# Last stage of a decode forward-and-backward kernel: last dq's products and output 1 ahead of the remaining dW units, dW spread evenly, K tiles reloaded first, later first wq load, padded rows

## The chip, the cores and the metric

One Trainium2 chip, one of its cores. The metric is the time of one execution on the device, in microseconds; a kernel's figure is the median of its runs. A small difference is read from a 95% interval; a kernel and the kernel before ran in the same rounds on the same chip. Each profile is of one run; its span is about 2 us shorter than that run's time.

## The reference, cut to what matters

```python
# two layers of attention with the same weights and caches, two MLPs between and after; one token, batch 2
x = x + attn(layernorm(x), k_cache, v_cache, wq, wo)      # caches [2, 4, 16384, 128], 32 query heads
x = x + mlp(layernorm(x), w1, b1, w2, b2)                 # 1024 -> 3584 -> 1024
x = x + attn(layernorm(x), k_cache, v_cache, wq, wo)
x = x + mlp(layernorm(x), w1, b1, w2, b2)
# outputs: x, and the gradients (vjp with grad_out) of x, k_cache, v_cache, wq, wo, w1, b1, w2, b2; all bf16
```

The big outputs are the gradients of both caches and of four weights. With one token, a weight gradient is an outer product of short rows: "dW" below. Output 1 is the gradient of x: two rows of 1024.

## The kernel before: the parts the change and the argument touch

The change is in the last stage, which begins at about 735 us: the backward pass of the first attention layer. It loads the caches again, computes ds and dq from them, and writes dK, dV and all dW. Its work is cut into steps `m`, two half-chunks of scores each. A step also takes some dW units from two queues, `fill` (MLP weights and wo) and `late` (wq). A unit is one matmul of 4 x 128 by 4 x 512, and one copy of its 128 x 512 result from PSUM into a tile ("home"); the last unit of a tile stores it.

```python
def load_tile():
    return (by_store or by_read).popleft()      # a tile whose store must land first, or one that was only read

def store(out_ap, view, tile_):
    nc.gpsimd.dma_start(out_ap, view)
    by_store.append(tile_)
# ... cut ...
fill.extend(dw_units(rowsA, rowsB, 2, list(w_chunks(HD, D)), 0, D, rows_of(out_5)))   # row group 2 of PE, last in fill
# ... cut ...
def step_fill(n):
    for k in range(n):
        for q in ((late, fill) if k % 2 == 0 else (fill, late)):
            if q and q[0].ready():
                q.popleft()()
                break

def fixed_tp(i):                                # a PSUM bank, zeroed by ACT
    t = pt([128, 8, 128], BF16, "tpm%d" % i)
    S.copy(out=t[:].bitcast(F32), in_=zero1[:].to_broadcast([128, 512]))
    return t
# ... cut: opening of the stage ...
TP.extend(fixed_tp(i) for i in range(2))
pump(NLD + 3, 4)
while 2 * m < NS + 12 or late or fill or late_pe or m <= max(v_at) + 2:
    # ... cut: transposes, scores, dK and dV pairs of the step ...
    step_fill(1 if m < NCH else 5)
    pump(NLD + 3 if m < NCH else NLD, 3)        # the next loads
    m += 1
g0 = attn_in_bwd(0, g1, dn0)                    # layer-norm backward, then output 1
col_to_row_f32(g0, DJ, out_1.rearrange("b s d -> (b s) d"), "o1")
```

## Time and profile before

| | before |
|---|---|
| median (lowest to highest) | 1144.22 us (1143.81 to 1147.24) |
| span of the profiled run | 1140.8 us |
| PE busy | 84% |
| bytes moved, mean rate | 449.3 MB, 394 GB/s |
| mean granted PE clock | 0.847 |

The page of the kernel before: busy tenths of PE's clock and of the DMA engines in 40 slices of 28.5 us, and the sum of the transfers.

```profile
PEclk9989785597999876999998899989779868896785
DMA  9999999998999989999999999887999999999996
DMA packets 89130, 449.30 MB, mean 394 GB/s; under 512 B 7026, under 2 KB 7026, under 8 KB 49788
```

The DMA engines are the limit nearly everywhere. The slices of lower share in the last stage are its opening (slices 26 to 28) and its end (the last). The same kernel, the busy time of each engine in stretches of the last stage; the last three columns are granted PE clock, DMA share and GB/s.

```profile
core 0: us, PE busy (x) PEld busy (x) DVE busy (x) ACT busy (x) POOL busy (x), PEclk, DMA share, GB/s
735.00:790.00 55.00, 45.87 (x777) 32.57 (x777) 41.15 (x77) 38.96 (x76) 5.92 (x11) 0.94 0.75 287
790.00:1110.00 320.00, 287.82 (x3682) 175.32 (x3680) 245.86 (x429) 228.93 (x440) 47.78 (x81) 0.80 1.02 420
1110.00:1120.00 10.00, 7.42 (x53) 3.79 (x52) 5.80 (x12) 4.89 (x9) 1.04 (x2) 0.50 0.83 348
1120.00:1130.00 10.00, 8.85 (x92) 3.96 (x92) 5.94 (x11) 6.06 (x11) 1.83 (x3) 0.50 0.50 206
1130.00:1140.00 10.00, 2.85 (x11) 1.19 (x10) 3.24 (x12) 0.68 (x2) 1.31 (x2) 0.50 0.59 237
```

There are three parts: an opening with holes, a full stretch at 420 GB/s, and a tail with holes, through which PE has half its clock. The holes of the tail do not mean that DMA had stopped being the limit. Each transfer adds 16 to a semaphore, one for each DMA engine (Trainium skill, "DMA: Bandwidth & Descriptors", Why a DMA increments its semaphore by 16 and not by 1: the engines finish independently, and only the full 16 means that all landed). Counting these increments in the trace, the store that was issued at 1111.86 us has its fifteenth at 1120.78 and its sixteenth at 1128.12; and stores land (sixteenth) at 1128.12, 1130.64, 1133.14, 1135.65 and 1138.13, every 2.5 us. I read this as one engine that is behind all others, works without a gap and ends the kernel; I call it the straggler. The 2.5 us agree with an engine at the common rate: a store is 1024 KB, so 64 KB for each of 16 engines, and at 420 / 16 GB/s that takes 2.5 us (an estimate).

The timeline of PE in the tail of the kernel before: start, length, group, and in brackets the idle time before it with what ended it.

```profile
1116.45 1.01 PE L1097 MATMUL tpm<-ident,dq_all 128*4 128x128 bf16 x8 [0.61 <-DVE dq_all L900]
...
1124.98 5.27 PE L1162 MATMUL xm<-rowsA,rowsB 4*128 4x512 bf16 x12 [0.49 <-ACT keepK L163]
...
1132.85 1.01 PE L200 MATMUL o<-identf,gA 128*2 128x128 f32 x4 [1.30 <-DVE gA L908]
1134.63 1.01 PE L200 MATMUL o<-identf,gA 128*2 128x128 f32 x4 [0.77 <-DVE o_row L201]
```

The last dq becomes rows at 1116.45, the last 12 dW units run at 0.44 us each, and output 1 comes after them, while the last stores still drain. And in the opening, PE waits for ACT's zeroing copy:

```profile
741.98 0.61 PE L1414 MATMUL tpm<-ident,keepxV 128*128 128x128 bf16 x8 [1.65 <-ACT tpm L1342]
```

### The profile page before, as it was taken

The numbers are of one execution on the slowest core, as the hardware profiler recorded it, in microseconds if no ns is written. First come the engines' busy times: TensorE is split into PE (matmuls) and PEld (weight loads), VectorE is DVE, ScalarE is ACT, GpSimd is POOL, SyncE is SP. The second block draws the span as 40 slices with busy tenths as digits, with TensorE's granted clock in tenths as the row PEclk, the third lists the DMA queues.
The fourth block names the chain that finished last, engine by engine and source line by source line (L and its number), as shares of the span: only waits on it lengthen the run. The fifth ranks groups of instructions, "written<-read, shape, count | busy, mean of one in ns | idle before, by whom it ended". The sixth has DMA issues, their size and how long they took to land. (4 is left out here: it accounts for less than half of the span.)

```text
span 1140.8 us, 39972 instructions
## 1 busy us (share of the span) xinstructions
PE 954.6 (84%) x17567; PEld 736.6 (65%) x17567; DVE 633.4 (56%) x1347; ACT 566.2 (50%) x1418; POOL 64.7 (6%) x117
## 2 busy tenths in 40 slices
PE   4988896487879885899987789988898989999885
PEld 3867674387767765888776688765555555555552
DVE  1535442133545433544845355768678868786784
ACT  0534351022535330344554444668677767776673
POOL 0000000000000000000000000001111112111111
PEclk9989785597999876999998899989779868896785
DMA  9999999998999989999999999887999999999996
GB/s 371 424 424 424 425 423 413 408 379 354 423 424 424 425 302 424 410 377 407 373 423 419 349 354 355 314 331 309 400 423 422 421 420 422 423 422 421 424 419 247
DMA packets 89130, 449.30 MB, mean 394 GB/s; under 512 B 7026, under 2 KB 7026, under 8 KB 49788
## 3 DMA queue, kind: packets, MB, share of 16 engines
q1 hardware_dynamic: 72204, 348.17, 75.4%
q0 software_dynamic: 16752, 98.59, 20.8%
q8 instruction: 137, 2.24, 0.7%
q14 instruction: 37, 0.30, 0.1%
HBM read 348.14 MB, written 98.58 MB: 392 GB/s over the span
## 5 line engine op out<-in xcount | busy, mean ns | idle before, releaser
L155 ACT COPY kT<-tp 128x512 int32<-128x512 int32 x209 | 122.8, 587 | 252.0 <-PE tp L421 243.3
L158 DVE COPY kT<-tp 128x1024 bf16<-128x1024 bf16 x159 | 108.6, 691 | 109.2 <-PE tp L421 97.3
L421 PE MATMUL tp<-ident,kv_K 128*128 128x128 bf16 x1728 | 144.5, 233 | 4.5 <-DMA kv_K<-in_A_k_cache_dram 4.4
L421 PEld LDWEIGHTS <-kv_K 128*128 128x128 bf16 x1728 | 109.6, 104 | 5.3 <-DMA kv_K<-in_A_k_cache_dram 5.2
L166 DVE CAST big<-xm 128x512 bf16<-128x512 f32 x135 | 88.1, 686 | 25.3 <-PE xm L1162 11.7
L163 ACT CAST big<-xm 128x512 bf16<-128x512 f32 x162 | 88.3, 594 | 24.6 <-PE xm L1162 12.7
L574 PEld LDWEIGHTS <-kT 128*128 128x128 bf16 x2048 | 76.6, 98 | 27.8 <-issue 21.4
L574 PE MATMUL sc<-qT_bf,kT 128*128 128x8 bf16 x2048 | 92.0, 171 | 0.3 <-issue 0.3
L538 ACT ACTIVATE e_all<-sc,negm 128x64 bf16<-128x64 f32 x256 | 77.1, 345 | 1.1 <-DVE negm L533 1.0
L307 PEld LDWEIGHTS <-wt 128*128 128x128 bf16 x1696 | 49.2, 104 | 43.7 <-issue 14.8
L421 PE MATMUL tp<-ident,kv_V 128*128 128x128 bf16 x864 | 70.1, 227 | 8.5 <-DMA kv_V<-in_A_v_cache_dram 7.6
L271 PE MATMUL wtp<-ident,wt 128*128 128x128 bf16 x928 | 73.9, 225 | 3.7 <-issue 2.5
L166 DVE CAST keepK<-xm 128x512 bf16<-128x512 f32 x91 | 59.1, 686 | 21.7 <-PE xm L1244 17.7
L453 PE MATMUL acc_all<-kv_V,e_all 128*16 128x256 bf16 x864 | 46.5, 296 | 26.4 <-DMA kv_V<-in_A_v_cache_dram 13.7
L163 ACT CAST keepK<-xm 128x512 bf16<-128x512 f32 x105 | 56.8, 594 | 23.8 <-PE xm L1244 23.1
L158 DVE COPY wT<-wtp 128x1024 bf16<-128x1024 bf16 (+1 forms) x64 | 40.7, 641 | 46.6 <-PE wtp L271 43.5
L155 ACT COPY wT<-wtp 128x512 int32<-128x512 int32 (+1 forms) x60 | 34.3, 572 | 61.7 <-PE wtp L271 47.5
L421 PEld LDWEIGHTS <-kv_V 128*128 128x128 bf16 x864 | 55.4, 102 | 10.7 <-DMA kv_V<-in_A_v_cache_dram 8.3
L166 DVE CAST keepV<-xm 128x512 bf16<-128x512 f32 (+1 forms) x80 | 52.5, 686 | 16.3 <-PE xm L1244 12.8
L163 ACT CAST keepV<-xm 128x512 bf16<-128x512 f32 (+1 forms) x93 | 50.3, 593 | 20.1 <-PE xm L1244 18.2
L538 ACT ACTIVATION_READ_ACCUMULATOR e_all<-sc,negm 128x1 f32 x256 | 60.1, 235 | 0.0
L271 PEld LDWEIGHTS <-wt 128*128 128x128 bf16 x928 | 56.3, 100 | 4.4 <-issue 3.0
(350 smaller groups left out, 1786.9 us busy)
## 6 DMA issues: line engine op xcount, KB each, us to landing
kv_K<-in_A_k_cache_dram SPq DMA_DIRECT2D x81, 1024.0 KB, 12.3
kv_V<-in_A_v_cache_dram SPq DMA_DIRECT2D x81, 1024.0 KB, 12.1
out_dram<-big POOLq DMA_DIRECT2D x36, 1024.0 KB, 18.5
wt<-in_A_wo_dram SPq DMA_DIRECT2D x32, 1024.0 KB, 10.2
wt<-in_B_w_dram SPq DMA_DIRECT2D x32, 896.0 KB, 14.2
out_dram<-keepK POOLq DMA_DIRECT2D x21, 1024.0 KB, 18.3
out_dram<-keepV POOLq DMA_DIRECT2D x19, 1024.0 KB, 15.0
wt<-in_A_wq_dram SPq DMA_DIRECT2D x16, 1024.0 KB, 9.0
```

What stands on the lines that cost most here:

```text
L155: S.copy(out=dst.bitcast(I32), in_=src.bitcast(I32))
L158: V.tensor_copy(out=dst, in_=src)
L163: S.copy(out=dst, in_=src)
L166: V.tensor_copy(out=dst, in_=src)
L271: PE.transpose(tp[:, o, :], wv[:, j, (o0 + o) * 128:(o0 + o + 1) * 128], ident[:])
L307: PE.matmul(fps[:, jo, :].rearrange("p (a b) -> p a b", b=2), lhsT=wv[:, j, jo * 128:(jo + 1) * 128], rhs=xT_bf[:, j0 + j, :].unsqueeze(1) ...
L421: PE.transpose(tp[:, j, :], cv[:, b * 8 + j, :], ident[:])
L453: PE.matmul(self.acc[cg:cg + 16, :], lhsT=coef(u), rhs=self.cv[:, t:t + 2, :].rearrange("p t d -> p (t d)"), start=False, stop=True, tile_ ...
L538: S.activation(out=e_all[:, g, f * half:(f + 1) * half, l, h, :], in_=sc[g][f][:, h, :].rearrange("p (a b) -> p a b", b=2), func=ACT.Exp, ...
L574: PE.matmul(sc[g][f][:, :, t % TH], lhsT=kT[:, j, :], rhs=q_bf[:, g, :], start=True, stop=True)
```

## The change: intent and diff

The intent: give the loads an earlier start in the opening (reload into K tiles, which no store holds; load wq later; drop two copies that PE waits for), and have dW units left to fill the tail's holes while the last quarter of dq goes to its products with wq and to output 1 first. The diff is cut to its core; instruction counts on PE are equal (17567 both).

```diff
+    opening = {"on": True}
     def load_tile():
-        return (by_store or by_read).popleft()
+        return (by_read or by_store if opening["on"] else by_store or by_read).popleft()
@@ loads of wq @@
-            if i % (2 * NCH) == NCH:
+            if i % (2 * NCH) == NCH + (2 if i < 2 * NCH else 0):
@@ last quarter: products with wq and output 1 at once, between the steps @@
+    def in_rows(q, kv):
+        # cut: two parts of 32 matmuls each, then layer-norm backward and output 1, one a half-step
     def quarter(kv):
         quarters[kv][1]()
-        late_pe.append(quarters[kv][3])
-        late.append(rows_unit({3: (dq_all, kv * 8)}, rowsA, kv * 8))
-        late.extend(dw_units(rowsB, rowsA, 3, [(0, 4), (4, 4)], kv * D, D,
+        if kv == order[-1] % HKV:
+            while late_pe:
+                late_pe.popleft()()
+            tail.extend(in_rows(quarters[kv], kv))
+        else:
+            late_pe.append(quarters[kv][3])
+        late.append(rows_unit({3: (dq_all, kv * 8, HQ)}, rowsA, kv * 8))
+        late.extend(dw_units(rowsB, rowsA, 3, [(0, 4), (4, 2), (6, 2)], kv * D, D,
@@ dW spread @@
-    def step_fill(n):
+    def step_fill(n, keep):
-                if q and q[0].ready():
+                if q and (q is late or len(q) > keep) and q[0].ready():
-        step_fill(1 if m < NCH else 5)
+        step_fill(1 if m < NCH else 3 if not late and 2 * m < NS else 5, 24 if 2 * m < NS else 0)
@@ opening @@
-    TP.extend(fixed_tp(i) for i in range(2))
+    TP.extend(pt([128, 8, 128], BF16, "tpm%d" % i) for i in range(2))
-    pump(NLD + 3, 4)
+    pump(NLD + 3, 3)
+    opening["on"] = False
@@ end @@
-    g0 = attn_in_bwd(0, g1, dn0)
-    col_to_row_f32(g0, DJ, out_1.rearrange("b s d -> (b s) d"), "o1")
# cut: tiles of columns padded by 7, so that 32 columns are transposed instead of 4;
# the last chunk's dq one slot earlier; late_pe popped sooner when over 6
```

## The prediction

> **What bounds the kernel now.** The page: DMA engines 90% busy or more in nearly every slice, 449.3 MB at a mean of 394 GB/s against about 424 when full; PE 84%. The change touches the last stage, from about 735 us. The windows view shows three parts there: 735 to 790, an opening with DMA share mostly 0.6 to 0.9 (229 to 367 GB/s); 790 to 1116, full (420 GB/s); and 1116 to 1138, a tail whose share falls to 0.06 from 1120 to 1125.
>
> 0.06 is one engine of 16. The trace's semaphore updates agree: from 1060 us on each store's last increment comes 6 to 13 us after its fifteenth. The last stores land at an even 2.5 us spacing up to 1138.1 us, straight through the stretch where the other engines are idle. So one straggling DMA engine has no gap from about 784 us to the end, and it ends the kernel. The Trainium skill ("DMA: Bandwidth & Descriptors", Latency and other measured facts) says that engines 7 and 15 are usually slower; the trace does not number engines, but one slow engine agrees.
>
> **What the change does.**
> - Tail: the last 24 dW units (3 MB) are held back until scores end; the last quarter's wq products and output 1 go ahead. In the before, PE and the copies stand in a chain of waits from 1104 to 1125, and 15 DMA engines idle about 6.5 us (from the GB/s of those slices). The change fills that. But the straggler is not idle there, and its bytes are unchanged. I expect the hole to vanish and little from it in the end time: 0 to 1 us, plus 0.2 us for the output-1 transfer, which now lands 0.2 us after the last big store.
> - Opening: four K/V reloads now go into K tiles, free after the dq products (736 to 740 us); before they queued behind stores (issued 740.7, 748.1, 748.6, 749.0). No DMA engine was busy for 5.1 us between 730 and 790, 2.3 of them before 750. The two bank-zeroing ACT copies go, worth the 1.65 us that PE waited at 742. Later loads still wait for stores, and compute limits the opening, so: 2 to 4 us.
> - Even spreading (3 units a step instead of 5): bytes unchanged; steps already DMA-bound (6.4 us each, against 5.5 when DMA was idle at 780). About 0.
> - Padding, memsets: 32 weight columns instead of 4, same matmul; eight small memsets under loads already queued. 0.
>
> **Prediction.** 1144.2 - 3 (opening) - 1 (tail) - 1 (fewer stalls) = 1139 us; 8 in 10 between 1130 and 1145. Faster by over 2%: 0.04; within 2%: 0.95; slower: 0.01. If the straggler did not count, the average engine's work would end the kernel near 1126 (an estimate), so 2% is nearly out of reach.
>
> **What would show it.** Right: DMA share near 1 until 2 to 3 us before the last landing; no 0.06 stretch; no PE wait on the zeroing copies; four loads issued before 742; the last stores again spaced 2.5 us, last increment several us after the fifteenth; output 1 stored before the last dW. Wrong: last stores landing within 1 us on all engines (straggler not the limit, gain 10 us or more); or compute issuing the last store only as its predecessors land (32 units in a row at 0.43 us each, PE at half clock), which ends later than the straggler.
>
> **What would make it wrong.** The straggler's extra work depending on how loads and stores overlap; the opening losing bytes with three units a step; PE throttled harder in the denser tail.

## The result, and the profile after

The changed kernel took 1147.25 us in the median (1145.53 to 1148.24, 4 runs); the kernel before, beside it, 1144.01 (1143.66 to 1147.24, 4 runs). The ratio is 1.002, with an interval of 0.9999 to 1.0042. A ratio is the mean time of one kernel's runs over that of the other's of the same rounds, so it is not quite the ratio of the two medians. The prediction was 1139, with 8 in 10 between 1130 and 1145: the measured time lies above that.

The page of the changed kernel, the same rows:

```profile
PEclk9988895597989975899998899998799688867965
DMA  8999999998999989999999999988999999999977
DMA packets 89194, 449.30 MB, mean 392 GB/s; under 512 B 7090, under 2 KB 7090, under 8 KB 49852
```

The bytes are the same; the two last slices have a lower share. The same stretches of the last stage, in the changed kernel:

```profile
735.00:790.00 55.00, 47.24 (x729) 32.20 (x726) 39.68 (x74) 36.79 (x71) 4.78 (x9) 0.88 0.84 321
790.00:1110.00 320.00, 276.89 (x3696) 168.75 (x3693) 239.62 (x427) 225.96 (x431) 48.24 (x82) 0.82 1.00 411
1110.00:1120.00 10.00, 7.89 (x99) 3.74 (x99) 6.28 (x13) 5.37 (x10) 1.30 (x2) 0.50 0.34 137
1120.00:1130.00 10.00, 7.70 (x31) 2.07 (x29) 7.95 (x17) 5.49 (x11) 2.56 (x4) 0.50 0.73 306
1130.00:1140.00 10.00, 7.42 (x18) 2.23 (x16) 6.23 (x10) 5.63 (x10) 3.00 (x4) 0.50 0.80 324
1140.00:1146.00 6.00, 0.00 (x0) 0.00 (x0) 0.00 (x0) 0.00 (x0) 0.00 (x0) 0.50 0.43 175
```

The opening moves more (321 GB/s for 287), as meant. The hole of the tail has not gone: it has moved ahead to 1110 to 1120 (137 GB/s), and after it DMA runs at 306 and 324 GB/s, below its 420, up to the end. PE in the tail of the changed kernel:

```profile
1106.83 1.03 PE L1101 MATMUL tpm<-ident,dq_all 128*32 128x128 bf16 x8 [0.62 <-DVE dq_all L904]
...
1123.84 1.01 PE L199 MATMUL o<-identf,gA 128*2 128x128 f32 x4 [0.77 <-DVE o L200]
1124.79 0.60 PE L1174 MATMUL xm<-rowsA,rowsB 4*128 4x512 bf16 x1
1124.79 0.60 PE L1174 MATMUL xm<-rowsB,rowsA 4*128 4x512 bf16 x1
...
1130.02 7.41 PE L1174 MATMUL xm<-rowsB,rowsA 4*128 4x512 bf16 x17
```

The dq rows come 9.6 us sooner than before and output 1 about 11 us sooner (1123.84 for 1134.63), but then 32 dW units are still to be done, from 1124.79 to 1137.43, the last 17 of them one after the other at 7.41 / 17 = 0.436 us. The chain that ended last says the same in one line:

```profile
1126.06 9.62 PE xm L1174 x24
```

The store counts show that the straggler is no longer the limit: it has caught up at 1116.76, and from there the sixteenth increment of every store follows the fifteenth within 0.12 us. No store was issued between 1106.25 and 1115.99; the last was issued at 1138.70 and landed at 1143.25. In the kernel before the last dW store was issued at 1131.17.

In the opening four loads are issued at 734.16 to 737.80, where before they were at 740.65 to 749.04 (about 1.5 us of this is that the stage begins sooner in this run). So the loss does not seem to be there; the traces put it at the end, and the experiments test that.

### The profile page after: what moved, and what is told of

Same layout as the page of the kernel before. It is cut to its first block, busy times and chain, and to the rows that moved or that the text cites. A ratio compares the mean times of both kernels' runs of the same rounds, so it can differ in the third digit from the quotient of the medians. Undisturbed runs are those within 1.5% of the kernel's fastest.

```text
span 1145.3 us, 40004 instructions
## 1 busy us (share of the span) xinstructions
PE 948.4 (83%) x17567; PEld 729.7 (64%) x17567; DVE 631.5 (55%) x1356; ACT 565.8 (49%) x1415; POOL 67.3 (6%) x121
## 4 chain that ended last, share of the span: by engine, by line
PE 49%; DMA 32%; DVE 9%; ACT 4%; issue 4%; POOL 0%; SPq 0%; POOLq 0%; DVEq 0%; ACTq 0%
DMA kv_V<-in_A_v_cache_dram 13%; PE tp L420 9%; PE wtp L270 5%; PE acc_all L452 4%; PE tpm L1445 4%; PE xm L1174 3%; PE xm L1256 3%; DMA wt<-in_A_wo_dram 3%; DMA kv_K<-in_A_k_cache_dram 3%; DMA wqt<-in_A_wq_dram 3%; PE turn L322 2%; PE sc L573 2%; DMA out_dram<-big 2%; DMA keepxV<-in_A_v_cache_dram 2%; PE dp L1311 2%
## 5 line engine op out<-in xcount | busy, mean ns | idle before, releaser
L161 ACT CAST big<-xm 128x512 bf16<-128x512 f32 x150 | 82.5, 593 | 33.6 <-PE xm L1256 16.5
L164 DVE CAST big<-xm 128x512 bf16<-128x512 f32 x124 | 80.6, 684 | 29.5 <-PE xm L1256 12.4
L164 DVE CAST keepV<-xm 128x512 bf16<-128x512 f32 (+1 forms) x106 | 68.9, 684 | 21.5 <-PE xm L1256 14.4
L270 PE MATMUL wtp<-ident,wt 128*128 128x128 bf16 x928 | 77.3, 232 | 3.7 <-issue 2.3
L161 ACT CAST keepV<-xm 128x512 bf16<-128x512 f32 (+1 forms) x115 | 62.3, 593 | 31.7 <-PE xm L1256 25.5
L306 PEld LDWEIGHTS <-wt 128*128 128x128 bf16 x1696 | 48.8, 103 | 43.8 <-issue 14.8
L452 PE MATMUL acc_all<-kv_V,e_all 128*16 128x256 bf16 x864 | 46.5, 295 | 26.5 <-DMA kv_V<-in_A_v_cache_dram 13.2
L270 PEld LDWEIGHTS <-wt 128*128 128x128 bf16 x928 | 59.1, 104 | 4.4 <-issue 3.1
L164 DVE CAST keepK<-xm 128x512 bf16<-128x512 f32 x77 | 49.8, 683 | 14.7 <-PE xm L1256 8.8
L1256 PEld LDWEIGHTS <-blk 32*128 32x128 bf16 x992 | 24.8, 95 | 47.6 <-issue 36.9
```

Of the source, the lines that this page charges most:

```text
L161: S.copy(out=dst, in_=src)
L164: V.tensor_copy(out=dst, in_=src)
L270: PE.transpose(tp[:, o, :], wv[:, j, (o0 + o) * 128:(o0 + o + 1) * 128], ident[:])
L306: PE.matmul(fps[:, jo, :].rearrange("p (a b) -> p a b", b=2), lhsT=wv[:, j, jo * 128:(jo + 1) * 128], rhs=xT_bf[:, j0 + j, :].unsqueeze(1) ...
L452: PE.matmul(self.acc[cg:cg + 16, :], lhsT=coef(u), rhs=self.cv[:, t:t + 2, :].rearrange("p t d -> p (t d)"), start=False, stop=True, tile_ ...
L1256: PE.matmul(pss[r][:, b * 256:(b + 1) * 256], lhsT=blk[32 * r:32 * r + 32, o + 2 * h + b, :], rhs=Qm[32 * r:32 * r + 32, :, :].rearrange(" ...
```

## The experiments

All are of five rounds; the change itself has four runs on each side. At a threshold of 2%, before_act is slower, opening_act is unclear, and all others count as the same as the kernel before; smaller differences are read from the intervals. The five rounds' kernel before took 1146.06, 1145.62, 1143.18 and 1142.41 us in the four batches, so only ratios are compared across batches; 0.001 is 1.1 us.

| run | what it is | median, us | ratio to before (95%) |
|---|---|---|---|
| the change | | 1147.25 | 1.0020 (0.9999 to 1.0042) |
| opening_only | opening and padding alone | 1141.48 | 0.9963 (0.9944 to 0.9982) |
| tail_only | the change without its earlier loads (zeroing copies still gone) | 1149.01 | 1.0026 (1.0010 to 1.0041) |
| pace5_keep0 | the change at 5 units a step | 1144.63 | 0.9997 (0.9975 to 1.0018) |
| pace5_keep24 | 5 a step, 24 held back | 1153.45 | 1.0066 (1.0040 to 1.0092) |
| pace_only | before at 3 units a step | 1146.56 | 1.0016 (0.9991 to 1.0041) |
| opening_pace | opening and 3 units a step | 1145.28 | 1.0022 (0.9997 to 1.0048) |
| pace2 | the change at 2 units a step | 1153.29 | 1.0097 (1.0064 to 1.0130) |
| keep0_chain_last | pace5_keep0, output 1 last again | 1143.54 | 0.9997 (0.9975 to 1.0019) |
| opening_zero | opening_only with the zeroing copies | 1146.94 | 1.0024 (1.0002 to 1.0046) |
| nozero_only | before without the zeroing copies | 1142.12 | 0.9990 (0.9972 to 1.0008) |
| after_mix | the change, three row groups dealt in turn | 1154.47 | 1.0076 (1.0050 to 1.0102) |
| after_mix2 | the same, bias units kept early | 1158.19 | 1.0130 (1.0107 to 1.0152) |
| before_act | before, stores on ACT's queue | 1176.54 | 1.0257 (1.0226 to 1.0287) |
| opening_act | opening_only, stores on ACT's queue | 1171.20 | 1.0227 (1.0199 to 1.0256) |
| opening_sp_tail | opening_only, last stores on SP's queue | 1141.27 | 0.9973 (0.9947 to 0.9999) |

### Which half loses: opening or tail

Theory A: the dW units left over make the tail longer than the straggler. Theory B: the loss is in the opening or the full stretch.

opening_only puts the old tail and pace behind the new opening:

```diff
-        step_fill(1 if m < NCH else 3 if not late and 2 * m < NS else 5, 24 if 2 * m < NS else 0)
+        step_fill(1 if m < NCH else 5, 0)
# and the last quarter, the wq stores of (0, 4), (4, 4), and output 1 as before
```

> The changed kernel's opening and padding alone: K tiles reloaded first, first wq load later, no zeroing copies, padded rows; tail and pacing as before. Theory A: a little faster than before, 1142 to 1143 us (from the straggler's backlog, which stands about 1.3 us earlier in the changed kernel), against the 3 us predicted. Theory B: as slow as the changed kernel, about 1147.

It has the lowest ratio: 1141.48 us, 0.9963, below both the kernel before and the change. Its last stores land at 2.5 us spacing again (1129.60, 1132.10, 1134.63, 1137.10), the last with 1.7 us between fifteenth and sixteenth: the straggler is the limit there.

tail_only is nearly its complement (the zeroing copies stay out in both):

```diff
-    opening = {"on": True}
+    opening = {"on": False}
# and the first wq load and pump as before
```

> The changed kernel with the opening of before (store tiles reloaded first, wq load at its old place; zeroing copies still gone). Theory A: loses the opening's gain and keeps the tail's loss: 1148 to 1149 us. Theory B (opening to blame): about 1144.

1149.01, ratio 1.0026, with the straggler caught up at 1118.2 and the last store issued at 1141.26. Theory A was close in both: 1141.48 for 1142 to 1143, 1149.01 for 1148 to 1149. Theory B falls: the half that it blames is the half that gains.

### How many units are left over

```diff
# pace5_keep0
-        step_fill(1 if m < NCH else 3 if not late and 2 * m < NS else 5, 24 if 2 * m < NS else 0)
+        step_fill(1 if m < NCH else 5, 0)
# pace5_keep24
+        step_fill(1 if m < NCH else 5, 24 if 2 * m < NS else 0)
```

> The changed kernel with the dW pacing of before (5 units a step, none held back); everything else of the change stays. Theory A (the tail is on PE: with 3 units a step 38 dW units are left when the scores end, 55 with the last quarter's, at 0.43 us each at half clock): only 17 units are left, the end goes back to the straggling DMA engine, about 1142.5 us, 4 to 5 below the changed kernel, and the last store's 16th increment again comes over 1 us after its 15th. Theory B (the loss lies in the opening or in the saturated stretch, the tail is innocent): stays at about 1147.

1144.63: no unit is left when the scores end, and the last store's sixteenth increment comes 1.12 us after its fifteenth, as theory A said. The gain is smaller than it said: the ratio, 0.9997, is 0.0023 below the change's (about 2.6 us for 4 to 5), with intervals that overlap, and it is not that of the opening alone. So this run by itself does not settle the matter.

> The changed kernel with 5 units a step, but 24 held back until scores end. Theory A: 41 units in the tail instead of 55, 14 x 0.43 = 6 us less PE there, so about 1141 to 1142 us (not below the straggler's end). Theory B: stays at about 1147. If holding back in itself costs, this one is slower than the run without it by 24 x 0.43 less what idle time it fills.

1153.45: theory A as I had put it missed this by over 11 us. The last case of the expectation is nearer: against pace5_keep0 it is slower by 0.0069, 7.9 us, of 24 x 0.43 = 10.3. Theory A had expected that 24 units would be a good filling for the hole. In the trace the hole stays (44 GB/s from 1120 to 1130), for two reasons. Ten of the units held back run before the dq rows, and the rows come late, at 1116.92 where pace5_keep0 has them at 1111.84 (part of these 5 us is older: its loads were 2 us later already at 730). PE in pace5_keep24:

```profile
1103.67 1.61 PE L1174 MATMUL xm<-rowsB,rowsA 4*128 4x512 bf16 x5
...
1109.22 2.31 PE L1174 MATMUL xm<-rowsB,rowsA 4*128 4x512 bf16 x5
...
1116.92 1.03 PE L1101 MATMUL tpm<-ident,dq_all 128*32 128x128 bf16 x8 [0.54 <-DVE dq_all L904]
```

And from the rows to the last landing of a dW store it takes 32.0 us (1116.92 to 1148.90), in pace5_keep0 26.4 (1111.84 to 1138.20). In the changed kernel, with 38 left, it is 36.4 (1106.83 to 1143.25).

```profile
1111.84 1.03 PE L1101 MATMUL tpm<-ident,dq_all 128*32 128x128 bf16 x8 [0.54 <-DVE dq_all L904]
```

Not all of these units run after the rows: in each of the two kernels ten of those left over run before. Counted in the traces, 16 units follow the rows in pace5_keep0, 30 in pace5_keep24 and 44 in the changed kernel. So 14 more cost 5.6 us and 28 more cost 10.1 us: 0.40 and 0.36 us for each. Units do not fill the hole for nothing, each is paid for.

The number left is not the whole of it: pace5_keep24 leaves fewer units over than the change and is slower (1.0066 for 1.0020). Its rows come at 1116.92, those of the change at 1106.83: the slower pace also makes the rows come sooner, and gives back part of what the tail costs.

A doubling should then show it far outside the spread:

```diff
# pace2
-        step_fill(1 if m < NCH else 3 if not late and 2 * m < NS else 5, 24 if 2 * m < NS else 0)
+        step_fill(1 if m < NCH else 2 if not late and 2 * m < NS else 5, 24 if 2 * m < NS else 0)
```

> The changed kernel with 2 dW units a step instead of 3. Counted while the program is built: 72 units are left when the scores end, instead of 38. Theory A (each unit left costs 0.3 to 0.44 us of copies and PE in the tail, less what the chain gains by starting earlier): 6 to 12 us slower than the changed kernel, about 1153 to 1159, with the last store issued 6 us or more later than the 1138.7 us there. If the tail is filled anyway (the units left cost nothing): within 2 us of the changed kernel.

Ratio 1.0097, 0.0077 above the change: about 8.8 us for 34 more units left, 0.26 us each (0.13 to 0.39, from the two intervals). The time fell in the range expected. Its last store was issued at 1141.29, only 2.6 us later than in the changed kernel, so that part missed; the profiled run was one of its fastest (span 1147.8; its runs lie between 1146.94 and 1160.48), so the 8.8 us do not show in this one trace. In it the rows come at 1096.23, 10.6 us sooner than in the changed kernel, and 78 units follow them; from the rows to the last landing it takes 49.6 us, 23.3 more than in pace5_keep0 for 62 more units, 0.38 us each. PE and DMA in the tail of pace2:

```profile
1110.00:1120.00 10.00, 8.59 (x32) 0.50 0.74 300
1120.00:1130.00 10.00, 10.00 (x25) 0.50 1.00 403
1130.00:1140.00 10.00, 10.00 (x25) 0.50 0.81 331
```

The same stretch in the timeline:

```profile
1118.44 21.93 PE L1174 MATMUL xm<-rowsB,rowsA 4*128 4x512 bf16 x51
```

For 22 us PE does nothing but 51 units of one row group, 21.93 / 51 = 0.43 us each, at half clock, and never idles.

### The pace or the reordering

pace_only has the change's `step_fill` and nothing else of it; opening_pace has the opening too.

```diff
# pace_only: on the kernel before
-        step_fill(1 if m < NCH else 5)
+        step_fill(1 if m < NCH else 3 if not late and 2 * m < NS else 5, 24 if 2 * m < NS else 0)
# opening_pace: the same edit on opening_only
```

> The kernel before with one thing of the change: 3 dW units a step instead of 5 while no late ones wait, and the keep of 24 (which never binds at that pace: 38 units are left when the scores end). Theory A (the change loses by the dW units that the slower pace leaves for the end, one after the other on PE at half clock): slower than the kernel before by 3 to 7 us, last stores landing on all engines within 1 us of one another, the last store issued after 1136 us. Rival B (the loss comes from the reordered last quarter and output 1, not from the pace): within 2 us of the kernel before, and the straggling engine still ends it, with lags of several us.

1.0016, between what the two theories had asked for; the time alone does not decide. The trace does: the stores issued from 1121.13 on land on all engines within 0.06 us of one another, the last dW store issued at 1135.78, so in this run the tail had turned from the straggler's to compute's, as A says.

> The opening and padding, and the pace of 3 a step (38 units left), but the last quarter, its stores and output 1 as in the kernel before. If the pace alone turns the opening's gain (ratio 0.9963) into the change's loss (1.002): 1.000 to 1.003. If the reordering does it: 0.996 to 0.998, like the opening alone. Output 1 comes last here, after all dW units.

1.0022, against 0.9963 for the opening alone and 1.0020 for the whole change. opening_pace differs from opening_only in the pace alone, by 0.0059 (0.0027 to 0.0091, about 6.7 us), and their intervals do not meet. In its trace the straggler has caught up at 1117.43, and the stores issued from 1118.55 on land on all engines within 0.09 us. So the pace by itself turns the opening's gain into the change's loss.

On the kernel before, the same pace cost only 0.0016. That fits an end that is the later of two, the straggler's and compute's: the opening moves the straggler's end, and once compute's is the later one, that gain no longer counts (with the pace, opening_pace is at 1.0022 beside pace_only's 1.0016, and tail_only, without the earlier loads, at 1.0026 beside the change's 1.0020). These differences lie inside the intervals, so this is argued and not shown.

Is the reordering free? keep0_chain_last has the products early but output 1 at the end, at 5 a step:

```diff
-            tail.append(lambda: col_to_row_f32(g0, DJ, out_1..., "o1", ...))
-        return [lambda: part(0), lambda: part(4), last]
+        ending.append(last)             # run after the loop; last() stores output 1 itself
+        return [lambda: part(0), lambda: part(4)]
```

> pace5_keep0 (1144.63) with the layer-norm backward and output 1 moved back behind all dW units; the last quarter's wq products still go at once. Theory C (output 1 first puts a chain of dependent waits ahead of the last dW units, where before it ran for free while the last stores drained): back to the opening alone, 1141 to 1142.5, last big store issued 3 to 4 us sooner than in pace5_keep0 (1134.0). Rival (the cost is in the early products and the smaller dWq stores): 1144 to 1145.

The last big store was issued at 1130.21, 3.8 us sooner than in pace5_keep0, as theory C said; but the time did not follow, 0.9997 both times. With the store sooner the straggler was the limit again (2.7 us between fifteenth and sixteenth at the end). So theory C is not borne out as a cause of time. Whether the reordering costs anything stays open: with the opening and 5 a step it measured +0.0034 (0.9963 to 0.9997, intervals that overlap), with 3 a step -0.0002.

### What the opening's gain is made of

```diff
# opening_zero: on opening_only
+        S.copy(out=t[:].bitcast(F32), in_=zero1[:].to_broadcast([128, 512]))      # for both banks
# nozero_only: on the kernel before
-    TP.extend(fixed_tp(i) for i in range(2))
+    TP.extend(pt([128, 8, 128], BF16, "tpm%d" % i) for i in range(2))
```

> The opening and padding alone (1141.5), with the two bank-zeroing ACT copies put back. Their share of the opening's gain of about 4 us: the prediction put 1.65 us of PE waiting on them. If they count fully: 1143. If the reloads into K tiles are all of it (DMA busy sooner, the copies hidden under them): 1141.5.

1.0024: the two copies, 0.6 us each on ACT, cost the opening its whole gain, and by the means more (0.0061, about 7 us, with intervals of 2 us on either side of each). The trace shows how a small delay grows. PE in opening_zero, the group that waits, and PE's busy time, clock, DMA share and GB/s after it:

```profile
743.94 0.61 PE L1452 MATMUL tpm<-ident,keepxV 128*128 128x128 bf16 x8 [1.65 <-ACT tpm L1379]
```

```profile
735.00:790.00 55.00, 47.34 (x703) 0.81 0.72 281
744.00:752.00 8.00, 7.68 (x90) 0.57 1.01 424
```

The same stretches of opening_only:

```profile
735.00:790.00 55.00, 47.63 (x771) 0.91 0.83 317
744.00:752.00 8.00, 7.39 (x144) 1.00 1.01 423
```

In these 8 us PE did 90 matmuls in the one and 144 in the other. In opening_only the first of these transposes stands at 742.33, 1.6 us sooner; by a later group of transposes (749.87 and 753.25) it is 3.4 us. The net loss of the wait is smaller than its 1.65 us, which I had overlooked: in opening_only PE waits 1.35 us for DVE right after its first group, so that the second group stands at 744.30 in the one and at 744.87 in the other, 0.6 us apart. The rest of the 3.4 us comes while the clock is at half.

```profile
744.30 0.62 PE L1445 MATMUL tpm<-ident,keepxV 128*128 128x128 bf16 x8 [1.35 <-DVE dl_rest L871]
744.87 0.84 PE L1452 MATMUL tpm<-ident,keepxV 128*128 128x128 bf16 x8 [0.32 <-ACT tpm L1379]
```
Both have the same loads in flight (issued 737 to 741 us), but the next store goes out at 756.13 in the one and at 759.51 in the other, and the DMA engines find less to do: no engine was busy for 2.9 us of 735 to 790 in opening_only, for 8.5 us in opening_zero. That the clock falls after idle time agrees with the Trainium skill ("TensorE: Matmul & The Clock Gate", What's actually happening), which says that the clock is either half or full and is set by how busy PE was over windows of about 3.4 us; here it fell to half for about 7 us, though the wait is shorter than such a window. The page calls the windows free-running, so that a wait of 1.65 us tips it may be a matter of phase. Over all 17 profiled kernels, the clock fell between 740 and 752 us in all four that have the copies (the kernel before, pace_only, opening_zero, before_act), and in two of the 13 that do not (the changed kernel, 0.72 from 740 to 744, and after_mix2, 0.57 from 744 to 748). So the copies go with the fall, but are not its only way. Nor does the clock tell the two kernels of this document apart: over 735 to 790 it is 0.94 in the kernel before and 0.91 in opening_only, whose clock falls later, from 772 to 788.

> The kernel before without its two bank-zeroing ACT copies; nothing else. In the trace of opening_zero the copies delayed the first transposes by 1.6 us, the PE clock then fell to half from about 744 to 752 us, and the steps were 3.4 us late by 753. If the copies are all of the opening's gain: ratio 0.995 to 0.998, and PE at full clock from 744 to 752. If the reloads into K tiles are needed as well: 0.999 to 1.001.

0.9990 (0.9972 to 1.0008), as expected if the reloads are needed as well. PE kept its full clock from 744 to 752 (the windows below), but the loads went out late as before, and DMA stood at 275 GB/s there. That the reloads make no gain while the copies stay is shown by opening_zero. That dropping the copies makes none without the reloads is less sure: the interval reaches to 0.9972 and meets that of opening_only (0.9944 to 0.9982), and over 735 to 790 DMA moved about as much as there (315 GB/s for 317). I think that the early reloads keep DMA fed only if compute is there to issue the stores that follow; this is argued and not shown.

```profile
735.00:790.00 55.00, 46.71 (x799) 0.91 0.80 315
744.00:752.00 8.00, 7.67 (x152) 1.00 0.75 275
```

### Does one row group limit the units

In the trace of the changed kernel units of different row groups start together (1124.79 twice), units of the same one do not. That agrees with the Trainium skill ("TensorE: Matmul & The Clock Gate", Why this matters for your kernels), which says that small-K matmuls in distinct row groups run concurrently. The copies of a unit, in the changed kernel from 1124 to 1139:

```profile
L161 ACT CAST big<-xm 128x512 bf16<-128x512 f32 x10 | 5.8, 586 | 2.0 <-PE xm L1174 2.0
L164 DVE CAST big<-xm 128x512 bf16<-128x512 f32 x10 | 6.8, 690 | 2.1 <-PE xm L1174 2.1
```

ACT and DVE together can take a unit every 1 / (1/0.586 + 1/0.690) = 0.317 us. So dealing the units among row groups should take the last stretch from 0.436 to 0.317 at best.

```diff
# after_mix: on the change
     units = [dw_units(rowsA, rowsB, 0, ...),
-            dw_units(rowsB, rowsA, 1, ...)]
+            dw_units(rowsB, rowsA, 1, ...),
+            dw_units(rowsA, rowsB, 2, list(w_chunks(HD, D)), 0, D, rows_of(out_5))]
# after_mix2: also the two bias units ahead of all dW units
```

> The changed kernel, but the dW units of the output projection are dealt among those of the two MLP weights, so that the 38 units left at the end come from three different row groups of PE in turn and no longer from one. Same number of units left, same bytes. If those units are limited by PE taking one row group at a time (17 of one group took 7.41 us, 0.44 us each, where two of different groups started together): 3 to 6 us faster than the changed kernel (1147.25), about 1142 to 1144, and the tail's DMA rate rises above 306 GB/s. If the tail is limited by the copies out of PSUM or by the homes coming free: within 1.5 us of the changed kernel.

> after_mix again without its confounder (there the two bias units, nine one-row matmuls, had slid to the very end and cost 4.4 us): here they come before all dW units. The dW units of three weights are dealt in turn, so of the 38 left when the scores end, 30 change row groups. In the changed kernel 17 units of one row group ran at 0.436 us each; ACT and DVE copies of 0.586 and 0.69 us allow 0.317 us a unit (worked out from those two). If PE's one-row-group runs limit the last stretch: 2 to 4 us faster than the changed kernel, 1143.5 to 1145.5, and the last store issued 2 to 3 us sooner after output 1 than the 12.8 us there. If not: 1147, same distance.

Both missed: 1.0076 and 1.0130, slower. In after_mix the nine bias matmuls had slid to the very end, at 4.4 us. after_mix2 mends that, and after output 1 it does 33 units in 12.1 us, 0.37 each, where the changed kernel did 32 in 12.6, 0.40 each; so the stretch itself ran a little faster, but by 1 us and not by the 2 to 4 expected. The changed kernel had already alternated in the first 15 of its 32 units, and after_mix2 still ends on nine of one group. But its dq rows come at 1116.68, 9.9 us later than in the changed kernel:

```profile
1116.68 1.04 PE L1101 MATMUL tpm<-ident,dq_all 128*32 128x128 bf16 x8 [0.54 <-DVE dq_all L904]
...
1142.57 3.99 PE L1174 MATMUL xm<-rowsB,rowsA 4*128 4x512 bf16 x9
```

Its transfers are slower in the opening (291 GB/s for 321) and the loads later from there. Three weights in turn keep three half-filled tiles instead of two, which could starve the loads of tiles; that is argued and not shown.

### The straggler and the store queue

```diff
 def store(out_ap, view, tile_):
-        nc.gpsimd.dma_start(out_ap, view)
+        nc.scalar.dma_start(out_ap, view)                          # before_act, opening_act
+        (nc.gpsimd if jobs else nc.sync).dma_start(out_ap, view)   # opening_sp_tail: SP once all loads are issued
```

The guess of the skill that the first expectation means is in "DMA: Bandwidth & Descriptors", Latency and other measured facts; it is told below. In the expectation of opening_sp_tail, "its lag" is that of the straggler.

> The kernel before with the big stores of the last stage issued by ACT's queue instead of GpSimd's. If the one straggling DMA engine is slow because of GpSimd's software-made descriptors (as the Trainium skill guesses): the last increment of the stores comes within 1 us of the fifteenth, the even 2.5 us spacing of the last landings goes, and the kernel ends when compute lets it, near 1133 to 1139 us. If that engine is slow whatever queue feeds it: same lags of 6 to 13 us and within 2 us of the kernel before. A third: ACT[...] issues stores late: slower, with holes in the DMA share between 790 and 1110.

> The opening and padding of the change alone (1141.5 us before), with the stores of the last stage on ACT's queue. Straggler tied to GpSimd's queue: 1130 to 1136, lags under 1 us. Straggler whatever queue: 1140 to 1143. If the gains of opening and queue don't add, because the opening's gain was only the straggler's earlier start: the same time as the kernel before with ACT's queue, within 1.5 us.

Both are about 30 us slower than the kernels that they are made from, but the lag is mostly gone, though not under the 1 us expected: from 900 us on, the sixteenth increment of a store comes at most 1.8 us (before_act) and 2.5 us (opening_act) after the fifteenth, where the kernel before has up to 13.0. (This is of the 33 and 31 stores whose increments could be counted; some share a semaphore with loads of which increments are missing.) So a lag of 6 to 13 us comes with GpSimd's queue here. It is not confined to GpSimd's stores: in the changed kernel two loads on SP's queue land whole 11.8 and 12.5 us after their fifteenth increment. And that a slower stream by itself keeps the lag small is not excluded, since both runs also move less. The Trainium skill's guess ("DMA: Bandwidth & Descriptors", Latency and other measured facts: engines 7 and 15 are usually slower, best guess contention at the descriptor rings of software-made transfers, and only for those) fits this as far as it goes; the trace does not number the engines. The price: in before_act from 900 to 1000 us the engines are as busy and move less, 400 GB/s for 422; the holes in the DMA share that the third case named do not show (1.00 from 790 to 1110). The kernel before, then before_act:

```profile
900.00:1000.00 100.00, 91.55 (x1122) 55.10 (x1120) 77.11 (x135) 71.85 (x139) 16.33 (x28) 0.79 1.02 422
900.00:1000.00 100.00, 87.06 (x1038) 50.62 (x1035) 71.96 (x123) 66.95 (x128) 0.00 (x0) 0.77 1.00 400
```

Why the same bytes keep the engines busy for longer there, I did not find out.

> The opening and padding alone (1141.5), with the stores issued after the last load (from about 1060 us on) put on SP's hardware queue, which then has no loads left. [...] If its lag no longer grows after the switch and the hole of 15 idle engines near 1120 lets it catch up: 1137 to 1140, lags under 3 us at the end. If its backlog at the switch decides: 1141 to 1142. If the switch slows the stream as on ACT's queue (400 GB/s for 422): slower, 1143 to 1146.

0.9973, the same as opening_only's 0.9963 within the spread. The last stores on SP's queue overtake: one issued at 1105.48 lands whole at 1118.59, one issued on GpSimd's queue at 1089.80 not before 1132.97, 15.5 us after its fifteenth increment. The last two stores, on SP's queue, still land 4.3 us after their fifteenth increment, at 1138.64 and 1141.15, again 2.5 us apart. This fits the second of the three expectations, that the backlog of the one engine decides, and a switch near the end came too late; the intervals do not part it from a small gain.

## Why the prediction was wrong, point by point

- "one straggling DMA engine ... ends the kernel": right for the kernel before, and for opening_only (landings 2.5 us apart to the end). The lags of 6 to 13 us hold there for the stores issued up to 1112 us; those of the last four are 2.1 to 1.4. In the changed kernel it had caught up at 1116.76, 26.5 us before the last landing.
- "Opening ... 2 to 4 us": the size was about right. opening_only gains 0.37%, 4.2 us (2.1 to 6.4). The sum behind it was not, so this was in part luck: I had added the reloads and the 1.65 us wait as two separate gains. Without the other, the reloads measured +0.24% and the dropped copies -0.10%; and in the trace the wait was worth 0.6 us net, which grew to 3.4 with PE at half clock.
- "Even spreading (3 units a step instead of 5): bytes unchanged ... About 0": **this is the step that failed.** I asked what the pace does to the stretch in which it acts, where DMA is the limit, and not how many units it leaves for the stretch after it, where DMA is not. It left 38, not the 24 that I took from `keep`, which never binds. pace_only gives +0.16% (its interval includes 0), opening_pace +0.22% against -0.37% without the pace, 0.59% or about 6.7 us (3.1 to 10.4); pace2 prices a unit left over at 0.26 us (0.13 to 0.39). Nor was the stretch before left as it was: the dq rows came sooner with fewer units a step.
- "I expect the hole to vanish and little from it in the end time: 0 to 1 us" of gain: wrong with it. The hole moved to 1110 to 1120 (137 GB/s), and the units came after it.
- The predicted sum with what was measured in place of its terms: 1144.2 - 4.2 (opening) + 6.7 (pace) = 1146.7, and 1147.25 was measured. The two terms sum to opening_pace by the way they were measured, so this checks only that the reordering adds little in this setting; on the kernel before the pace cost 0.16%, so the terms do not simply add.
- What I had written down as the sign of being wrong, "compute issuing the last store only as its predecessors land (32 units in a row at 0.43 us each, PE at half clock), which ends later than the straggler", is what happened, in size too: 32 units after output 1, the last 17 at 0.436 us, clock 0.50. I had the number in hand and priced it at nothing, since I took the straggler for a fixed end. It is only an end as long as compute issues the last store early enough: 1131.17 before, 1138.70 after.
- "Padding ...: 0" was not tested alone.
- Of the signs written down for being right, those of the program came (no wait on the zeroing copies, four loads before 742, output 1 stored before the last dW); those of the end did not (DMA share near 1 to the end, last stores 2.5 us apart with the last increment several us late).

The lowest ratio of the kernels run is opening_only's, 0.9963 of the kernel before (1141.48 us); opening_sp_tail, at 0.9973 (1141.27 us), is the same within the spread.

## What to carry to other kernels

Where one resource has no gap to the end, count when the last work is handed to it before you hold work back: work that is deferred past a saturated stretch is paid at the rate of the tail, here 0.36 to 0.40 us for each unit after the dq rows at half clock, of which the sooner rows gave back only a part, and not at that of the idle resource it was meant to fill. Count what a pacing rule really leaves over by building the program, for a limit in the code may never bind. And a short wait of PE can cost more than its length, if the clock falls after it: in the one pair of traces compared here 0.6 us net became 3.4.

## What the Trainium skill lacked or had wrong

- "DMA: Bandwidth & Descriptors", Latency and other measured facts: the slow engine is named there without a size. Here one engine's share of a store landed up to 13.0 us after the other fifteen with GpSimd's queue, and at most 2.5 us after them with ACT's. The section does not say that the engine may be behind without being slower: the last landings, 2.5 us apart, are those of an engine at the common rate (estimate above), and they ended the kernel.
- The same page: no section read says that stores on ACT's queue beside loads on SP's may move fewer bytes at the same busy share. Here it was 400 GB/s for 422 from 900 to 1000 us, both at a share of 1.0 or more, and 30 us in all.
- "TensorE: Matmul & The Clock Gate", What's actually happening: it gives one idle window of about 3.4 us as the way to half clock. Here a wait of 1.64 or 1.65 us was followed by 6 to 7 us at half clock in three kernels (clock 0.61 from 744 to 752 in the kernel before, 0.57 in opening_zero, and in pace_only), and one of 2.52 us in before_act by a fall as well. With a wait of 1.35 us in its place, the clock stayed at 1.00 from 740 to 752 in 11 of 13. Transposes stand around these waits; whether they count as busy for the clock was not tested, and if they do not, the page's window may still hold.
- The same page, What's actually happening: "K is binary" and half or full agrees: the clock records of all 17 traces hold 0.5 and 1.0 alone. In the tail, PE had half its clock through twenty microseconds in which it counted as busy 10.00 of every 10 (pace2, 1120 to 1140; the ends of matmuls are modelled in these views). This stream of matmuls with four rows in use did not release it, which the page does not say; why it did not is open.
